# The second pair's v loaded later, behind W1's second piece, and its cast shared by GpSimd and VectorE

## The chip, the cores and the metric

The kernel runs on one core of a Trainium2 chip. The metric is the device time of one execution in microseconds (us); lower is better. TensorE (PE in the profile) multiplies matrices, VectorE (DVE), ScalarE (ACT) and GpSimd (POOL) work on elements, and the core's 16 DMA engines move data between its memories and HBM. Two DMA queues matter here. Loads that SyncE (SP) issues run on the queue that the profile calls q1; loads that GpSimd issues, here those of the weights with a cast from f32 to a 2-byte type on the way, run on q0.

## The reference

A block-wise linear attention with a decay per head, then a normalisation and a two-layer MLP with a residual. B = 4, H = 8 heads, S = 768, D = 64; the MLP goes from 512 to 2048 and back.

```python
for b in range(S // 64):                       # attention, blocks of 64 positions
    intra = (qb @ kb^T) * Dmask                # Dmask[i, j] = lam ** (i - j) where i >= j
    out[:, :, sl] = intra @ vb + (qb * lam_pow) @ kv_state
    kv_state = lam ** 64 * kv_state + (kb * rev_pow)^T @ vb
x = out as (B, S, H * D)
xn = (x - mean) / sqrt(var + 1e-06) * g_ln
result = x + relu(xn @ w_ch1) @ w_ch2
```

## The kernel before

The 4 x 768 positions are cut into 12 windows of 256 positions, `u` = 0 to 11, each one belonging to one batch. The order of all work is written out by hand, and every engine takes its instructions in that order; waits between engines and on DMAs come from what the instructions read and write.

For a window, `load_in` brings q, k and v (512 KB each, as f32 rows of 512 bytes) into buffers, three of each kind. `in_k`, `in_q` and `in_v` turn them into bf16: k is cast, q and v are multiplied by powers of lam and cast. `in_q` with a slice of heads works in two halves, j = 0 and 1, one instruction each (L236). `in_v` is one instruction (L252). `HA` is heads 0 to 3 and `HB` is heads 4 to 7. TensorE then transposes q and k (`transpose_pe`, L260), forms the masked scores (`scores`, L289, masked by VectorE at L299), the products of k with v (`kv`, L333, output `pk`), the outputs of scores and state (`av`, L452, and `inter`, L465, output `po`). `norm` and `to_xT` centre and transpose the result (`xT`).

The first MLP layer takes W1 in four pieces (`load_w1(0)` to `(3)`, L127, issued by GpSimd; 512 KB each as it is stored, in bf16), the second W2 in four pieces (`load_w2`, L130). `m1a.tile(0, i)` uses W1's piece 0 (L689); `m1s(m1a, c, lo, hi)` uses piece c (L571). `m2a(i, part)` uses W2's piece `part` (L715). ScalarE takes the results with a ReLU (`hT`).

The stretch that the change touches runs from about 12 to 24 us. In it, in the order of the program:

- VectorE finishes the masks of window 0, writes one column of window 1's v buffer (the memset of L816), and SyncE then issues window 1's v load (L817): the memset is a gate, since the load writes over the same buffer and so waits for it.
- GpSimd waits on ScalarE's cast of window 1's k (`behind`, L776), issues W1's piece 1 (L894), takes window 1's q for HA (L895), issues pieces 2 and 3 (L897, L898), then casts window 1's v for all heads (L899).
- VectorE takes window 1's q for HB (L896) in two halves, normalises window 0, and masks window 1's scores (L913, L916).
- TensorE runs `m1a.tile(0, 0)`, window 1's scores, `m1a.tile(0, 1)`, the first half of `m1s(m1a, 1)` at L921, which needs W1's piece 1, and then `kv(1)` at L929, which needs window 1's v in bf16.
- ScalarE writes one column of window 2's k buffer (L922), which gates SyncE's loads of window 2's k, q and v; GpSimd's second `behind` (L926) waits for that k to land and then issues W2's pieces.

Of the kernel before, what the change touches and what calls it, by code (L numbers as in the profile page):

```python
# [17 lines left out]
def kernel(  # L18
# [11 lines left out]
    nc = tc.nc  # L30
# [45 lines left out]
    qkv_in = {}  # L76
# [5 lines left out]
    def fill(got, name, u, hs, eng=None):  # L82
        eng = eng or nc.sync
        src = dict(k=k, q=q, v=v)[name]
        if u < LB:
            eng.dma_start(got[:, hs], source(src, u, hs))
            return
        cc, b = divmod(u, B)
        for j in range(2):
            eng.dma_start(got[:, hs, j * D:(j + 1) * D],  # L90
                          src[b, hs, cc * W + j * C:cc * W + (j + 1) * C, :].rearrange("h p d -> p h d"))
# [6 lines left out]
    def open_in(u, gate):  # L98
        qkv_in[u] = {name: inp.tile([128, H, 2 * D], F32, tag=name + "in", name=name + "in") for name in "kqv"}
        if gate:  # L100
            nc.gpsimd.memset(qkv_in[u]["k"][:, 0, 0:1], 0.0)

    def load_in(u, name, eng):
        got = qkv_in[u][name]
        fill(got, name, u, slice(0, H), eng)
        qkv_in[u][name] = got.rearrange("p h (j d) -> p h j d", j=2)
# [19 lines left out]
    def load_w1(c):  # L126
        nc.gpsimd.dma_start(w1[c], moe_w_ch1[:, c * W1C:(c + 1) * W1C].rearrange("(k p) f -> p k f", p=128))  # L127
# [80 lines left out]
    def open_window(u):  # L208
        kq = wk.tile([128, 2, NP, 2, 2, D], BF16, tag="kq", bufs=3, name="kq")
        vb = wk.tile([128, H, 2, D], BF16, tag="vb", bufs=4, name="vb")  # L210
        st[u] = dict(kq=kq, vb=vb)
        if u < XB:
            st[u]["kqT"] = wk.tile([128, 2, NP, 2, 128], BF16, tag="kqT", bufs=3, name="kqT")

    def part(a, dst, hs):

        return dst[:, a, hs.start // 2:hs.stop // 2].rearrange("p a j e d -> p a e j d")

    ALL = slice(0, H)

    def in_k(u, eng, hs=ALL):
        src = qkv_in[u]["k"][:, hs].rearrange("p (a e) j d -> p a e j d", e=2)
        dst = part(0, st[u]["kq"], hs)
        for j in range(2):
            (eng.copy if eng is nc.scalar else eng.tensor_copy)(dst[:, :, :, j], src[:, :, :, j])

    def in_q(u, eng, hs=ALL):
        src = qkv_in[u]["q"][:, hs].rearrange("p (a e) j d -> p a e j d", e=2)
        dst = part(1, st[u]["kq"], hs)
        if u < LB:  # L230
            lq = lam_q[:, hs, :].rearrange("p (a e) j -> p a e j", e=2)
        else:
            lq = lam_p[:, 0:1, hs].rearrange("p j (a e) -> p a e j", e=2).to_broadcast([128, (hs.stop - hs.start) // 2, 2, 2])
        n = (hs.stop - hs.start) // 2
        for j in range(2):
            eng.tensor_tensor(dst[:, :, :, j], src[:, :, :, j],  # L236
                              lq[:, :, :, j:j + 1].to_broadcast([128, n, 2, D]), op=ALU.mult)

    def in_k_one(u, eng, j):
        src = qkv_in[u]["k"].rearrange("p (a e) j d -> p a e j d", e=2)  # L240
        (eng.copy if eng is nc.scalar else eng.tensor_copy)(part(0, st[u]["kq"], ALL)[:, :, :, j], src[:, :, :, j])  # L241
# [7 lines left out]
    def in_v(u, eng, hs=ALL):  # L249
        n = hs.stop - hs.start  # L250
        lv = lam_v[:, hs, :, None] if u < LB else lam_p[:, 1, hs, None, None]
        eng.tensor_tensor(st[u]["vb"][:, hs], qkv_in[u]["v"][:, hs], lv.to_broadcast([128, n, 2, D]), op=ALU.mult)  # L252
# [23 lines left out]
    def scores(u, hf, early=False):  # L276

        s = st[u]
        kT, qT = s["kqT"][:, 0], s["kqT"][:, 1]
        if early:  # L280
            sc = [mm_tile([128, 2, 2, 128], F32, f"sce{e}") for e in range(2)]
        else:
            sc = [bank([128, 2, 2, 128], F32, "sc", f"sc{e}") for e in range(2)]
        mA = wk.tile([128, 2, 2, 2, 128], BF16, tag=f"mA{hf}", name=f"mA{hf}")
        for i in range(2):
            for jk in range(2):
                for ab in range(2):
                    for e in range(2):
                        nc.tensor.matmul(sc[e][half[ab], i, jk, :], lhsT=kT[half[e], 2 * hf + i, jk, half[ab]],  # L289
                                         rhs=qT[half[e], 2 * hf + i, :, half[ab]],  # L290
                                         start=(i == 0 and jk == 0), stop=(i == 1 and jk == 1), skip_group_check=True)
        s[f"mA{hf}"] = mA
        s[f"sc{hf}"] = sc

    def mask(u, hf, heads=(0, 1)):
        s = st[u]
        kp = keep.rearrange("p a b t -> p a (b t)")
        for e in heads:
            nc.vector.tensor_tensor(s[f"mA{hf}"][:, e], s[f"sc{hf}"][e],  # L299
                                    kp[:, None, :, :].to_broadcast([128, 2, 2, 128]), op=ALU.mult)  # L300

    def mask_by_act(u, hf):

        s = st[u]
        for e in range(2):
            nc.scalar.copy(s[f"mA{hf}"][:, e], s[f"sc{hf}"][e])
        kp = keep_h.rearrange("p a b t -> p a (b t)")
        for e in range(2):
            m = s[f"mA{hf}"][:, e]
            nc.vector.tensor_tensor(m, m, kp[:, None, :, :].to_broadcast([128, 2, 2, 128]), op=ALU.mult)  # L310

    def fill_pe(n, tag, wide=False):
        t = bank([128, 128], F32, tag, "unread")
        for i in range(n):
            if wide:
                nc.tensor.matmul(t, lhsT=warm, rhs=warm, start=True, stop=True)
            else:
                nc.tensor.matmul(t[half[i % 2], 0:D], lhsT=warm[half[0], half[i % 2]], rhs=warm[half[0], half[0]],
                                 start=True, stop=True, skip_group_check=True)

    def kv(u, tag="mm", between=None):

        s = st[u]
        cc, b = divmod(u, B)
        n_ab = 2 if (cc + 1) * W < S else 1
        pk = [bank([128, 2, NP, D], F32, f"po{ab}" if tag == "po" else tag, f"pk{ab}")[:, 0] for ab in range(n_ab)]
        for p in range(NP):
            if p == NP // 2 and between:
                between()
            for j in range(2):  # L330
                for e in range(2):
                    for ab in range(n_ab):
                        nc.tensor.matmul(pk[ab][half[e], p, :], lhsT=s["kq"][half[ab], 0, p, j, e],  # L333
                                         rhs=s["vb"][half[ab], 2 * p + e, j],
                                         start=(p == 0 and j == 0), stop=(p == NP - 1 and j == 1), skip_group_check=True)
        s["pk"] = pk
# [434 lines left out]
    HA, HB = slice(0, 4), slice(4, 8)  # L771
# [24 lines left out]
    nc.vector.tensor_copy(e_p[:, 0:1], io_p)  # L796
    nc.vector.tensor_scalar(e_p[:, 1:2], e_p[:, 0:1], -1.0, None, op0=ALU.mult)
    in_q(0, nc.vector, HA)
    in_k(0, nc.gpsimd, HB)
    load_w1(0)  # L800
    in_q(0, nc.vector, HB)
    transpose_pe(0, 1, (0, 1))
    transpose_pe(0, 0, (2, 3), nc.vector)
# [9 lines left out]
    fill_pe(6, "po0")  # L813
    scores(0, 1, early=True)
    mask_by_act(0, 1)
    nc.vector.memset(qkv_in[1]["v"][:, 0, 0:1], 0.0)  # L816
    load_in(1, "v", nc.sync)  # L817
    kv(0, between=lambda: fill_pe(8, "po0"))
    new_state(0, 0, nc.scalar)
    av(0, (0, 1))  # L820
# [46 lines left out]
    def wind_down(u, abs=(0, 1)):  # L867
# [7 lines left out]
        for ab in abs:  # L875
            x, xh = s["x"][:, ab], s["x"][:, ab].rearrange("p (a e d) -> p a e d", e=2, d=D)
            nc.scalar.copy(x, s["po"][ab].rearrange("p h d -> p (h d)"))
            if has[ab]:
# [7 lines left out]
            nc.vector.scalar_tensor_tensor(s["xc"][:, ab], in0=x, scalar=s["mv"][:, ab, 0:1], in1=g_row,  # L886
                                           op0=ALU.subtract, op1=ALU.mult)

    open_window(1)
    in_k(1, nc.scalar)  # L890
    norm(0, 0, early=True)
    reader(0)
    behind(st[1]["kq"][:, 0, 0, 0, 0, 0:1])
    load_w1(1)  # L894
    in_q(1, nc.gpsimd, HA)  # L895
    in_q(1, nc.vector, HB)  # L896
    load_w1(2)  # L897
    load_w1(3)  # L898
    in_v(1, nc.gpsimd)  # L899
    open_in(2, False)  # L900
    fill_pe(5, "sc", True)
    transpose_pe(1, 0, (0, 1))
# [11 lines left out]
    to_xT(0, 1)  # L914
    scores(1, 1, early=True)
    mask(1, 1)  # L916
    for i in range(2):
        nc.scalar.activation(lam_p[:, i], lnlam, ACT.Exp, scale=e_p[:, i:i + 1])
    keep_x(0, nc.scalar.copy)
# [604 lines left out]
```

## Time and profile before

| | |
|---|---|
| time, median of 3 runs | 205.96 us (205.44 to 205.98) |
| the profiled execution's own time | 205.75 us |
| its span, first to last instruction | 204.0 us |
| TensorE busy | 194.7 us, 95% |
| VectorE, ScalarE, GpSimd busy | 142.7, 121.6 and 89.6 us |
| HBM read and written | 27.27 and 6.29 MB |

The profile is of one execution. All points in time below are microseconds from the first instruction, so 1.75 us of the execution's own time lie outside the span. The granted TensorE clock is 1.000 in the whole span. A row of the timeline gives start, duration, engine, line, operation, output and inputs, sizes, and the count of instructions merged into it; a bracket gives the idle time of the engine before it and what ended it. A row of the waits gives in total how long, how often and at most how long one line waited for another. A row of a DMA queue gives its packets, megabytes and the time of its packets as a share of the 16 engines' time in the stretch asked for; since packets overlap, a busy queue can exceed 100%. An issue row ends with the time from issue to landing.

### The profile page before, as it was taken

The page shows a single profiled execution, that of the slowest core. Times are in us where ns is not written, and L with a number is a line of the kernel's source. Part 1 is how long each engine was busy: PE and PEld are TensorE (multiplying, and loading weights), DVE is VectorE, ACT ScalarE, POOL GpSimd, SP SyncE. Part 2 cuts the span into 40 slices and gives each one's busy share as a digit, 9 for nine tenths or more (in the row PEclk, how much of TensorE's full clock was granted, in tenths as well). Part 3 has the DMA queues.
Part 4 walks back from the last instruction along what each step waited for, and adds up shares of the span by engine and source line. Part 5 has one row for each costly group of instructions (what it writes and reads, how often), then busy time and mean ns, then how long its engine had stood idle before and what let it go on. Part 6 is the DMA issues. An engine that isn't in the chain of part 4 may idle for free.

```text
span 204.0 us, 7526 instructions
## 1 busy us (share of the span) xinstructions
PE 194.7 (95%) x3223; PEld 163.0 (80%) x3223; DVE 142.7 (70%) x298; ACT 121.6 (60%) x285; POOL 89.6 (44%) x125
## 2 busy tenths in 40 slices
PE   1998999999999999999999999999999999999992
PEld 0487798645777889889899888888888888888881
DVE  3588372779799879879686576866856577955372
ACT  3787678555425767656596386584484592852720
POOL 5557049301964790863673962644436303001010
PEclk9999999999999999999999999999999999999999
DMA  4999999999989899799699995999989865110703
GB/s 105 302 255 219 217 301 194 196 248 253 231 179 208 186 268 187 156 201 150 145 200 203 210 209 96 213 234 131 190 158 151 249 192 132 29 26 2 203 11 97
DMA packets 93747, 36.41 MB, mean 178 GB/s; under 512 B 71313, under 2 KB 91281, under 8 KB 93714
## 3 DMA queue, kind: packets, MB, share of 16 engines
q1 hardware_dynamic: 88624, 29.96, 69.6%
q0 software_dynamic: 4704, 5.77, 15.4%
q8 instruction: 25, 0.41, 0.8%
q10 hardware_dynamic: 386, 0.20, 0.4%
q14 instruction: 8, 0.07, 0.1%
HBM read 27.27 MB, written 6.29 MB: 164 GB/s over the span
## 4 chain that ended last, share of the span: by engine, by line
PE 77%; DMA 12%; DVE 5%; ACT 3%; POOL 2%; issue 1%; DVEq 0%
PE pm L571 31%; DMA w<-in_moe_w_ch_dram 10%; PE pwd L606 9%; PE pwc L606 9%; PE pwa L606 8%; PE pm1t L689 4%; PE pwb L606 4%; PE pm L715 3%; DMA lam_b<-in_lam_dram 2%; PE po L465 1%; PE po L439 1%; DVE mA L299 1%; PE sc L379 1%; DVE hs L591 1%; PE po L452 1%; PE pk L398 1%
## 5 line engine op out<-in xcount | busy, mean ns | idle before, releaser
L571 PE MATMUL pm<-xT,w 128*128 128x256 bf16 x656 | 76.2, 273 | 0.3 <-DMA w<-in_moe_w_ch_dram 0.3
L571 PEld LDWEIGHTS <-w 128*128 128x128 bf16 x656 | 62.8, 98 | 8.6 <-DMA w<-in_moe_w_ch_dram 0.5
L574 ACT ACTIVATE hT<-pm 128x512 f16<-128x512 f32 x82 | 47.8, 596 | 30.0 <-PE pm L571 28.5
L606 PEld LDWEIGHTS <-hs 128*128 128x128 f16 x320 | 31.1, 98 | 3.6
L631 POOL TENSOR_TENSOR x<-ev_u,x 128x256 f32<-128x256 f32 x10 | 7.4, 742 | 60.4 <-ACT ev_u L630 60.4
L606 PEld LDWEIGHTS <-hT 128*128 128x128 f16 x240 | 23.2, 98 | 2.7
L589 DVE TENSOR_TENSOR hs<-hT 128x1024 f16<-128x1024 f16 x20 | 14.3, 717 | 14.7 <-ACT hT L574 13.5
L508 DVE SCALAR_TENSOR_TENSOR xc<-po,nmean,g_row 128x512 bf16<-128x512 f32 x18 | 13.2, 742 | 5.5 <-ACT nmean L492 5.5
L339 POOL TENSOR_TENSOR Sn<-Stmp,lam_s 128x256 bf16<-128x256 f32 x16 | 10.0, 627 | 13.4 <-DVE Stmp L419 5.6
L715 PE MATMUL pm<-w,hT 128*128 128x512 f16 x64 | 15.1, 379 | 0.1
L491 ACT ACTIVATE x<-po 128x512 f32<-128x512 f32 x18 | 10.7, 594 | 6.6 <-PE po L465 3.7
L689 PE MATMUL pm1t<-xT,w 128*128 128x128 bf16 x224 | 13.7, 219 | 0.6 <-ACT xT L532 0.3
L619 DVE SCALAR_TENSOR_TENSOR x<-pwd,rstd,x 128x256 f32<-128x256 f32 x20 | 9.7, 483 | 6.4 <-POOL x L642 3.4
L689 PEld LDWEIGHTS <-w 128*128 128x128 bf16 x224 | 12.9, 98 | 1.1 <-DMA w<-in_moe_w_ch_dram 0.5
L252 POOL TENSOR_TENSOR vb<-vin,lam_p 128x1024 bf16<-128x1024 f32 x7 | 13.3, 1897 | 0.0
L246 POOL TENSOR_TENSOR kq<-qin,lam_p 128x512 bf16<-128x512 f32 x11 | 11.4, 1043 | 3.8 <-PE pm L571 2.6
L539 ACT ACTIVATE sq<-x,nmean 128x512 bf16<-128x512 f32 x18 | 12.9, 718 | 0.1
L606 PE MATMUL pwa<-w,hT 128*128 128x256 f16 x80 | 12.0, 273 | 0.0
L619 DVE SCALAR_TENSOR_TENSOR x<-pwa,rstd,x 128x512 f32<-128x512 f32 (+1 forms) x20 | 11.5, 611 | 0.7
L606 PE MATMUL pwb<-w,hT 128*128 128x256 f16 x80 | 11.5, 273 | 0.0
L606 PE MATMUL pwd<-w,hs 128*128 128x256 f16 x80 | 11.2, 273 | 0.0
L241 POOL CAST kq<-kin 128x512 bf16<-128x512 f32 x9 | 5.8, 655 | 11.8 <-DMA kin<-in_k_dram 10.6
(139 smaller groups left out, 336.4 us busy)
## 6 DMA issues: line engine op xcount, KB each, us to landing
kin<-in_k_dram SPq DMA_DIRECT2D x16, 256.0 KB, 5.0
qin<-in_q_dram SPq DMA_DIRECT2D x16, 256.0 KB, 4.4
vin<-in_v_dram SPq DMA_DIRECT2D x16, 256.0 KB, 5.1
w<-in_moe_w_ch_dram POOLq DMA_DIRECT2D x8, 512.0 KB, 9.2
out_dram<-x SPq DMA_DIRECT2D x16, 256.0 KB, 4.4
kin<-in_k_dram SPq DMA_DIRECT2D x4, 512.0 KB, 9.7
qin<-in_q_dram SPq DMA_DIRECT2D x4, 512.0 KB, 6.7
vin<-in_v_dram SPq DMA_DIRECT2D x4, 512.0 KB, 7.8
```

Of the source, the lines that this page charges most:

```text
L246: eng.tensor_tensor(part(1, st[u]["kq"], ALL)[:, :, :, j], src[:, :, :, j], lq[:, :, :, None].to_broadcast([128, NP, 2, D]), op=ALU.mult)
L252: eng.tensor_tensor(st[u]["vb"][:, hs], qkv_in[u]["v"][:, hs], lv.to_broadcast([128, n, 2, D]), op=ALU.mult)
L491: nc.scalar.activation(x, po, ACT.Copy, accum_out=sm)
L508: nc.vector.scalar_tensor_tensor(s["xc"][:, ab], in0=po, scalar=s["nmean"][:, ab:ab + 1], in1=g_row, op0=ALU.add, op1=ALU.mult)
L539: nc.scalar.activation(sq, s["x"][:, ab], ACT.Square, bias=s["nmean"][:, ab:ab + 1], accum_out=s["ss"][:, ab:ab + 1])
L571: nc.tensor.matmul(pm[:, b, :], lhsT=w1[n // W2K][:, kk, (n % W2K) * 128:(n % W2K + 1) * 128], rhs=xT_of[g][:, kk, 0:N], start=(b == 0 and ...
L574: nc.scalar.activation(hT[:, u * NB:(u + 1) * NB, 0:N], pm, ACT.Relu)
L589: nc.vector.tensor_tensor(s13, b[:, :, 1:2, :].to_broadcast([128, n, 2, 128]), b[:, :, 0:4:3, :], op=ALU.subtract)
L606: nc.tensor.matmul(pr[bank], lhsT=lhs(r), rhs=rhs, start=(first and r == 0), stop=(r == KB // 2 - 1), skip_group_check=True)
L619: nc.vector.scalar_tensor_tensor(out, in0=in0, scalar=r[ab], in1=in1, op0=ALU.mult, op1=ALU.add)
L689: nc.tensor.matmul(pm[:, b, :], lhsT=w1[c][:, kk, b * 128:(b + 1) * 128], rhs=xT_of[g][:, kk, i * 128:(i + 1) * 128], start=(b == 0 and kk ...
L715: nc.tensor.matmul(acc[i], lhsT=hT[:, kk, i * 128:(i + 1) * 128], rhs=w2[kk // W2K][:, kk % W2K, :], start=(kk == 0), stop=(kk == KB - 1))
```

## The change

The v load of window 1 moves from behind VectorE's last mask of window 0 into the middle of VectorE's `in_q(1)` for HB, memset and load together: `in_q` gets a parameter that is called after its first half. `in_v(1)` on GpSimd is cut to HA and stays where it was; HB goes to VectorE, behind the second mask of window 1.

```diff
-    def in_q(u, eng, hs=ALL):
+    def in_q(u, eng, hs=ALL, after_first=None):
...
         for j in range(2):
             eng.tensor_tensor(dst[:, :, :, j], src[:, :, :, j],
                               lq[:, :, :, j:j + 1].to_broadcast([128, n, 2, D]), op=ALU.mult)
+            if j == 0 and after_first:
+                after_first()
...
     mask_by_act(0, 1)
-    nc.vector.memset(qkv_in[1]["v"][:, 0, 0:1], 0.0)
-    load_in(1, "v", nc.sync)
     kv(0, between=lambda: fill_pe(8, "po0"))
...
+    def late_v():
+
+        nc.vector.memset(qkv_in[1]["v"][:, 0, 0:1], 0.0)
+        load_in(1, "v", nc.sync)
+
     open_window(1)
...
     load_w1(1)
     in_q(1, nc.gpsimd, HA)
-    in_q(1, nc.vector, HB)
+    in_q(1, nc.vector, HB, after_first=late_v)
     load_w1(2)
     load_w1(3)
-    in_v(1, nc.gpsimd)
+    in_v(1, nc.gpsimd, HA)
...
     scores(1, 1, early=True)
     mask(1, 1)
+    in_v(1, nc.vector, HB)
     for i in range(2):
```

## The prediction

> **What bounds the kernel now.** The first view is the list of what TensorE waited for in the whole span, since TensorE is busy for 95% of it.
>
> ```profile
> ...
> PE pm L571 <- DMA w<-in_moe_w_ch_dram: 0.3, 1, 0.3
> PE pm1t L689 <- ACT xT L532: 0.3, 1, 0.3
> PE pm1t L689 <- ACT kqT L261: 0.2, 1, 0.2
> ```
>
> After its start TensorE has three waits, 0.8 us together. They all lie in the stretch that the change touches, as TensorE's timeline shows:
>
> ```profile
> 16.95 1.10 PE L689 MATMUL pm1t<-xT,w 128*128 128x128 bf16 x16 [0.24 <-ACT kqT L261]
> ...
> 19.39 1.05 PE L689 MATMUL pm1t<-xT,w 128*128 128x128 bf16 x16 [0.33 <-ACT xT L532]
> 20.78 1.05 PE L571 MATMUL pm<-xT,w 128*128 128x256 bf16 x8 [0.34 <-DMA w<-in_moe_w_ch_dram]
> 21.76 0.45 PE L333 MATMUL pk<-vb,kq 64*64 64x64 bf16 x32
> ```
>
> At 20.78 it waited 0.34 us for W1's piece 1, and kv(1) at 21.76 follows with no wait. That 0.34 us is what an earlier piece 1 can win here. The chain that ended last shows a second place where weights arrive as TensorE wants them:
>
> ```profile
> 13.39 7.35 DMA w<-in_moe_w_ch_dram
> ...
> 31.26 12.88 DMA w<-in_moe_w_ch_dram
> 44.14 0.04 issue
> 44.18 1.02 PE pm L715 x4
> ```
>
> W2's piece 2, issued at 31.26, lands at 44.14, and the product that needs it starts at 44.18. How long TensorE stood there is seen by comparing two equal groups in its timeline:
>
> ```profile
> 41.00 1.90 PE L715 MATMUL pm<-w,hT 128*128 128x512 f16 x8
> ...
> 43.07 2.13 PE L715 MATMUL pm<-w,hT 128*128 128x512 f16 x8
> ```
>
> The second takes 0.23 us more, the pause at 44.18. So a delay of TensorE before 44 us costs its length less 0.23, and a gain before 44 us is lost unless W2's piece 2 comes earlier too. Behind it TensorE has no wait that the list shows, so what is left goes to the end in full.
>
> **Who holds what in the stretch.** The other engines' timelines:
>
> ```profile
> 12.15 0.06 DVE L816 MEMSET vin<- 128x1 f32 x1
> 12.83 0.70 DVE L497 BATCH_NORM_STATS2 stats<-po 128x6 f32<-128x512 f32 x1 [0.62 <-PE po L452]
> ...
> 14.64 0.49 DVE L236 TENSOR_TENSOR kq<-qin,lam_q 128x256 bf16<-128x256 f32 x1
> ...
> 18.43 1.29 DVE L299 TENSOR_TENSOR mA<-sc,keep 128x512 bf16<-128x512 f32 x2 [0.48 <-PE sc L289]
> 19.64 1.28 DVE L299 TENSOR_TENSOR mA<-sce,keep 128x512 bf16<-128x512 f32 x2
> 24.07 0.17 DVE L476 COPY seen<-po 128x8 f32<-128x8 f32 x1 [3.15 <-PE po L465]
> ```
> ```profile
> 8.02 0.94 POOL L127 DMA_DIRECT2D w<-in_moe_w_ch_dram  x1
> ...
> 13.39 0.80 POOL L127 DMA_DIRECT2D w<-in_moe_w_ch_dram  x1
> 14.21 1.39 POOL L236 TENSOR_TENSOR kq<-qin,lam_q 128x256 bf16<-128x256 f32 x2
> 15.55 1.54 POOL L127 DMA_DIRECT2D w<-in_moe_w_ch_dram  x2
> 18.49 1.90 POOL L252 TENSOR_TENSOR vb<-vin,lam_v 128x1024 bf16<-128x1024 f32 x1 [1.40 <-DMA vin<-in_v_dram]
> 28.07 0.35 POOL L776 COPY seen_p<-kin 128x1 f32<-128x1 f32 x1 [7.67 <-ACT hT L574]
> ```
> ```profile
> 12.25 0.37 SPq L86 DMA_DIRECT2D vin<-in_v_dram  x1
> 22.57 0.37 SPq L86 DMA_DIRECT2D kin<-in_k_dram  x1
> ```
>
> v was issued at 12.25, was there at about 18.4, and was cast from 18.49 to 20.39. kv(1) took it at 21.76, so v has 1.37 us of slack now.
>
> **Part 1, the gate.** The memset (0.06 us) leaves 12.15; VectorE idles for TensorE until 12.83 anyway, so nothing is won. It comes back after the half that ends at 14.64 + 0.49 = 15.13. VectorE has no gap from there until it idles 0.48 us before 18.43, which hides 0.06 us; uncovered it would cost 0.06. SyncE issues v at about 15.2 instead of 12.25, 2.95 us later. On SyncE's queue the next load is at 22.57, so none is pushed back.
>
> **Part 2, when v lands.** This is the term that decides. Three loads share the DMA engines. From issue to landing, piece 0 (issued at 8.02), piece 2 (at 15.55):
>
> ```profile
> w<-in_moe_w_ch_dram POOLq DMA_DIRECT2D x1, 512.0 KB, 8.9
> ...
> w<-in_moe_w_ch_dram POOLq DMA_DIRECT2D x1, 512.0 KB, 7.7
> ```
>
> Piece 0 landed at 16.9, v at 18.4, piece 1 at 13.39 + 7.35 = 20.74, piece 2 at 23.25. On the DMA engine that ends last, the loads follow one another: v costs 18.4 - 16.9 = 1.5 us and piece 1 costs 20.74 - 18.4 = 2.3 us. That they are served in the order of issue, not shared, is seen in the two queues from 17 to 18 us, when piece 1 was long issued:
>
> ```profile
> q0 software_dynamic: 182, 0.19, 112.8%
> q1 hardware_dynamic: 38, 0.02, 6.3%
> ```
>
> 6.3% is one engine of 16, given wholly to v: 0.063 x 16 us / 38 = 27 ns a packet. Now the later stretch from 39 to 43 us, where both queues had much waiting:
>
> ```profile
> q0 software_dynamic: 559, 0.56, 82.7%
> q1 hardware_dynamic: 547, 0.28, 34.6%
> ```
>
> There the queues move packet for packet, and a packet of q1 takes 0.346 x 64 us / 547 = 40 ns. So both ways exist in this trace. I take the order of issue, since the situation is the nearest: the same v, the same pieces of W1, one behind the other. Then piece 1, issued before v, goes first: it lands at 16.9 + 2.3 = 19.2 and v at 19.2 + 1.5 = 20.7. Piece 0's landing, and with it the start at 16.95, stays. The bounds, from the times to landing of all loads of v up to 60 us:
>
> ```profile
> DMA to landing us min/median/max: 5.1/6.2/14.2
> ```
>
> That is 20.3 at the earliest and 29.4 at the latest (the 14.2 us load ran into W2's four pieces). From 15 to 15.75 us q0 did almost nothing:
>
> ```profile
> q0 software_dynamic: 9, 0.01, 5.4%
> ```
>
> Unless piece 1 was only kept out by v, engines that have finished piece 0 now stand still there for up to 0.75 us. Piece 2 lands with 0.7 us in hand before TensorE's next piece of work at about 24, and the engine that ends last has no hole, so I cost this at nothing.
>
> **Part 3, the cast.** The nearest rows are GpSimd's two halves of window 0's v, and VectorE's multiply of the same size:
>
> ```profile
> 8.98 2.06 POOL L252 TENSOR_TENSOR vb<-vin,lam_v 128x512 bf16<-128x512 f32 x2
> ```
> ```profile
> 8.00 0.76 DVE L236 TENSOR_TENSOR kq<-qin,lam_q 128x256 bf16<-128x256 f32 x2 [0.53 <-DMA qin<-in_q_dram]
> 14.64 1.24 DVE L236 TENSOR_TENSOR kq<-qin,lam_q 128x256 bf16<-128x256 f32 x2
> 29.71 0.69 DVE L246 TENSOR_TENSOR kq<-qin,lam_q 128x512 bf16<-128x512 f32 x1 [1.00 <-DMA qin<-in_q_dram]
> ```
>
> HA on GpSimd costs 1.03 us alone. HB on VectorE costs 0.69 alone. Both now run at the same time, and the pair of L236 took 1.24 us beside GpSimd's L236 against 0.76 without it. So HB lies between 0.69 and 0.69 x 1.24 / 0.76 = 1.13, and HA between 1.03 and, with the same 0.48 us, 1.51. I take 1.15 for HA, near the lower end, because the overlap is shorter than HA. VectorE is free at 20.92, so HB ends between 21.6 and 22.1. HA starts 0.1 after the landing: 20.8 + 1.15 = 21.95, and kv(1) can start at about 22.05.
>
> The waits that are added hold up little. Behind HA on GpSimd stands L776, which waits for a load until 28.07. Behind HB on VectorE stands L476 at 24.07, which waits for TensorE's po. ScalarE's gate for window 2's k stands behind the ReLU of L921, not behind kv(1), so W2's loads keep their time.
>
> **The sum.** TensorE could reach kv(1) at 21.76 - 0.34 = 21.42, and the bf16 v lets it start at 22.05: 0.29 us later than before. The pause of 0.23 at 44.18 takes most of it: +0.06. From the profiled execution's 205.75 this gives 205.8; the median of the runs stands 0.21 above that execution, so I forecast 206.0. With HA at its ends and the landing 0.4 us either way, kv(1) starts between 21.5 and 22.8, and the change lies between -0.25 and +0.8: this case's own range is 205.6 to 206.8.
>
> **The rivals.**
>
> *The queues share packet for packet* (slower). Pieces 2 and 3, issued at 15.55 to 17.1, keep q0 full while v runs. By the rows of 39 to 43 us q1 moves 547 packets in 4 us, 137 a us; v has 1024 (512 KB in rows of 512 bytes), 7.5 us. The load issued at 22.57 had its first packets between 23.5 and 23.75:
>
> ```profile
> q1 hardware_dynamic: 20, 0.01, 13.2%
> ```
>
> So from 1.0 us behind its issue, at 16.2, v can run; it ends at 23.7, lands at about 24.2, and kv(1) starts at 25.4: +3.6, less 0.23, gives 209.3 against the median. It decides as soon as W1's piece 2 is taken up before v's packets are. For it: the 39 to 43 rows. Against it: the one engine at 17 to 18 us. The Trainium skill, page "DMA: Bandwidth & Descriptors", section "Queues, rings and completion order", says that each DMA engine goes round between the queues that have work, a packet at a time. By that rule the time would be this rival's; the trace agrees from 39 to 43 us and not at 17 to 18 us.
>
> *Part of v is caught.* If a quarter to a half of v's 64 packets on an engine are paired with piece 2, each costs 4 us x 16 / 547 = 117 ns instead of 27, so 1.4 to 2.9 us more: 207.4 to 208.9, in the middle 208.
>
> *The gain is real.* v lands at 20.3 or sooner, kv(1) starts at 21.42, and W2's piece 2 also comes 0.2 us or more earlier: -0.34 to -0.57, 205.4 to 205.6; if the waits at 16.95 and 19.39 (0.57 together) shrink too, down to 205.0. For it: one DMA engine sets each landing, and the others end sooner. Against it: W2's pieces do not hang on this stretch.
>
> **How the numbers follow.** Forecast 0.50, full sharing 0.16, partial 0.16, gain 0.18. About 0.3%, 0.6 us, is what a measurement can tell from no change. Of the forecast 0.04 lies above that bound, of the gain 0.12 below it. So faster 0.12, within 0.3% 0.46 + 0.06 = 0.52, slower 0.32 + 0.04 = 0.36. The range goes from 205.2 to 208.7, which leaves out most of full sharing and the far end of the gain.
>
> **What would show it.** L571's wait for w at 20.78 gone, its start at about 20.4; GpSimd's half of L252 starting at 20.8; kv(1) at 22.05 with a wait for vb; the pause at 44.18 gone. Wrong if q0 and q1 move equal counts of packets from 18 to 23 us, or if v lands before 20.3.

## The result, and the profile after

| | before | after |
|---|---|---|
| median of 6 runs each | 205.70 us (205.38 to 208.14) | 215.82 us (214.05 to 216.69) |
| profiled execution, its own time | 205.75 | 214.35 |
| its span | 204.0 | 212.6 |
| TensorE's mean granted clock | 1.000 | 0.983 |

The change makes the kernel 4.6% slower: the ratio is 1.0459, with a 95% interval of 1.039 to 1.0527. The forecast was 206.0 us, with 208.7 as the upper end of its range. Ratios here and below leave disturbed runs out; that matters for one experiment, e7, where it drops the four slowest of nine runs although their lower clock may be the edit's own effect.

The two profiled spans differ by 8.6 us. The page of after starts with the span, each engine's busy time, and the granted clock in 40 slices:

```profile
span 212.6 us, 7527 instructions
...
PE 197.0 (93%) x3223; PEld 164.5 (77%) x3223; DVE 146.1 (69%) x299; ACT 121.8 (57%) x285; POOL 88.6 (42%) x125
...
PEclk9999859999999999999999999999999999999999
```

TensorE does the same 3223 instructions but is busy 2.3 us longer (194.7 before), and two slices, from 21 to 32 us, show a lower clock. VectorE is busy 3.4 us longer (142.7 before) with one instruction more. Both are signs that something other than a wait was added. The waits come next, TensorE's list after its start (total, times, longest):

```profile
PE pk L335 <- POOL vb L254: 4.1, 1, 4.1
PE pm L573 <- DVE x L741: 2.8, 1, 2.8
```

Neither wait is in the list of before. The wait for W1's piece 1, which the change was to shorten, is gone. TensorE's timeline of after shows the first one (start, length, engine, line, operation, and in brackets the wait ahead of it):

```profile
20.58 1.04 PE L573 MATMUL pm<-xT,w 128*128 128x256 bf16 x8
25.74 0.64 PE L335 MATMUL pk<-vb,kq 64*64 64x64 bf16 x32 [4.12 <-POOL vb L254]
26.32 1.89 PE L573 MATMUL pm<-xT,w 128*128 128x256 bf16 x8
...
31.51 1.05 PE L573 MATMUL pm<-xT,w 128*128 128x256 bf16 x8
```

The group that was L571 now starts at 20.58 with no wait, 0.20 earlier. kv(1) starts at 25.74 instead of 21.76: **3.98 us of the loss**. Then eight products of L573 take 1.89 us, where eight of the same size take 1.04 at 20.58 and 1.05 at 31.51. The granted clock says why, in two stretches of after (stretch, its length, TensorE's busy time and instructions, granted clock, DMA share, GB/s):

```profile
21.50:24.60 3.10, 0.12 (x2) 1.00 1.24 208
24.60:31.40 6.80, 5.66 (x128) 0.50 1.16 295
```

From 24.6 us, 1.1 us ahead of the end of the pause, the granted clock is half for 6.8 us. What that costs is read where it ends. The L573 group at 31.51 stood at 25.18 before, as the first of these rows of before's timeline shows:

```profile
25.18 1.05 PE L571 MATMUL pm<-xT,w 128*128 128x256 bf16 x8
...
45.04 0.39 PE L531 MATMUL xt<-ident,xc 128*128 128x128 bf16 x4
...
54.17 3.62 PE L715 MATMUL pm<-w,hT 128*128 128x512 f16 x16
```

31.51 - 25.18 = 6.33, so the clock adds 6.33 - 3.98 = **2.35 us**. The Trainium skill, page "TensorE: Matmul & The Clock Gate", section "Why this matters for your kernels", warns of idle gaps of over about 3 us between matmul bursts, after which TensorE falls back to half clock; this trace agrees, with 4.12 us of idling and a clock of 0.50.

The same groups further on, in after:

```profile
49.40 1.90 PE L717 MATMUL pm<-w,hT 128*128 128x512 f16 x8
51.14 0.39 PE L533 MATMUL xt<-ident,xc 128*128 128x128 bf16 x4
...
60.58 2.78 PE L573 MATMUL pm<-xT,w 128*128 128x256 bf16 x24 [2.77 <-DVE x L741]
63.19 3.62 PE L717 MATMUL pm<-w,hT 128*128 128x512 f16 x16
```

The group of L717 at 49.40 stood at 43.07 and took 2.13; now it takes 1.90. The pause of **0.23** for W2's piece 2 is gone, and the transposes behind it are 51.14 - 45.04 = 6.10 late. But the group at 63.19 is 63.19 - 54.17 = 9.02 late, so another 9.02 - 6.10 = **2.92 us** is lost in between, nearly all of it in the 2.77 us wait for VectorE's x. VectorE's timeline of after, ahead of that x:

```profile
51.50 0.83 DVE L840 TENSOR_TENSOR wt<-w 128x512 f16<-128x512 f16 x1
52.36 1.15 DVE L842 TENSOR_TENSOR wt<-w,wt 128x512 f16<-128x512 f16 x1
...
55.82 2.12 DVE L840 TENSOR_TENSOR wt<-w 128x512 f16<-128x512 f16 x1
57.97 0.42 DVE L842 TENSOR_TENSOR wt<-w,wt 128x512 f16<-128x512 f16 x1
...
59.78 0.75 DVE L741 SCALAR_TENSOR_TENSOR x<-pm,rstd,x 128x512 f32<-128x512 f32 x1
```

These are additions of W2's rows, in two groups, and before the same two groups took 0.41 to 0.43 us an addition. The rows that answer to the first two, in VectorE's timeline of before:

```profile
45.14 0.42 DVE L840 TENSOR_TENSOR wt<-w 128x512 f16<-128x512 f16 x1
45.59 0.42 DVE L842 TENSOR_TENSOR wt<-w,wt 128x512 f16<-128x512 f16 x1
```

What lies beside them is GpSimd's work, in its timeline of after and then of before:

```profile
50.69 1.36 POOL L243 CAST kq<-kin 128x512 bf16<-128x512 f32 x2 [2.59 <-DMA kin<-in_k_dram]
52.01 3.60 POOL L248 TENSOR_TENSOR kq<-qin,lam_q 128x512 bf16<-128x512 f32 x3
55.58 2.08 POOL L254 TENSOR_TENSOR vb<-vin,lam_v 128x1024 bf16<-128x1024 f32 x1
```
```profile
51.19 1.36 POOL L241 CAST kq<-kin 128x512 bf16<-128x512 f32 x2 [2.27 <-DMA kin<-in_k_dram]
52.51 3.68 POOL L246 TENSOR_TENSOR kq<-qin,lam_q 128x512 bf16<-128x512 f32 x3
```

GpSimd's multiplies start at about 52 us in both kernels, right behind casts of k that wait for a load of k. VectorE's additions moved from 45 to 51.5 us and now run into these casts and multiplies, and slow down from 0.42 to as much as 2.12 us; the first one after GpSimd's cast of v ends, at 57.66, takes 0.42 again. The Trainium skill, page "SBUF — State Buffer", section "SBUF: two separate sides", says that VectorE and GpSimd share a pair of ports, held by one instruction at a time, when VectorE has two inputs in SBUF; these rows agree, and say how much it is here.

The four terms, 3.98 + 2.35 - 0.23 + 2.92, give 9.02 up to that group by construction, and the span grew by 8.6. Most of the other 0.4 comes back soon behind it: the 64 small products of L452 take 1.00 us at 62.15 in before, and the same ones (L454) take 0.71 at 71.06 in after.

**Why v came late.** The issues of v and of W1, and the first reader of v, are in the timelines of SyncE and of GpSimd, both of after:

```profile
15.12 0.37 SPq L86 DMA_DIRECT2D vin<-in_v_dram  x1
```
```profile
13.32 0.80 POOL L127 DMA_DIRECT2D w<-in_moe_w_ch_dram  x1
...
15.49 1.54 POOL L127 DMA_DIRECT2D w<-in_moe_w_ch_dram  x2
24.21 1.48 POOL L254 TENSOR_TENSOR vb<-vin,lam_v 128x512 bf16<-128x512 f32 x1 [7.18 <-DMA vin<-in_v_dram]
```

v is issued at 15.12, as forecast. It has landed by 24.1, not 20.7. Piece 1, issued 1.8 us ahead of v, did go first, as forecast: from 15 to 18 us q0 moves 411 packets and q1 none, and piece 1 lands 6.5 us behind its issue, at 19.8. The DMA queues of after, packets, MB and share of the engines' time, first from 19 to 20 us and then from 20.75 to 21.5 us:

```profile
q1 hardware_dynamic: 529, 0.27, 90.0%
q0 software_dynamic: 37, 0.03, 20.7%
```
```profile
q0 software_dynamic: 129, 0.13, 104.6%
q1 hardware_dynamic: 45, 0.02, 15.0%
```

In the first stretch v (q1) has nearly all engines to itself, and a packet takes 0.90 x 16 us / 529 = 27 ns. That is half of v's 1024 packets within one microsecond. In the second, W1's pieces 2 and 3 (q0) move and some of v's last packets go in between at 0.15 x 16 x 0.75 us / 45 = 40 ns each. These are the two rates that before showed: 27 ns for a load that an engine serves alone, 40 ns for one that is served in turn with q0. So v isn't shared as a whole, nor served wholly in order: most of it goes at once, and a remainder is paired with piece 2, which was issued 0.37 us behind it. On this reading, which no view shows directly, an engine that has taken v up before piece 2 arrives moves it whole, and the others go in turn. The experiments shift that distance.

### The profile page after: what moved, and what is told of

It is laid out like the page before. It is cut to its first block, busy times and chain, and to the rows that moved or that the text cites. A ratio compares the mean times of both kernels' runs of the same rounds, so it can differ in the third digit from the quotient of the medians.

```text
span 212.6 us, 7527 instructions
## 1 busy us (share of the span) xinstructions
PE 197.0 (93%) x3223; PEld 164.5 (77%) x3223; DVE 146.1 (69%) x299; ACT 121.8 (57%) x285; POOL 88.6 (42%) x125
## 4 chain that ended last, share of the span: by engine, by line
PE 84%; DVE 6%; DMA 5%; ACT 1%; POOL 1%; issue 0%; ACTq 0%; POOLq 0%
PE pm L573 34%; PE pwd L608 8%; PE pwa L608 8%; PE pwc L608 8%; PE pm1t L691 5%; DMA vin<-in_v_dram 4%; PE pwb L608 4%; PE pm L717 4%; PE po L454 2%; PE po L467 2%; PE tp L262 2%; DVE wt L840 1%; DMA g_one<-in_moe_g_ln_dram 1%; PE po L441 1%; PE sc L381 1%; PE pk L335 1%
## 5 line engine op out<-in xcount | busy, mean ns | idle before, releaser
L573 PE MATMUL pm<-xT,w 128*128 128x256 bf16 x656 | 78.0, 276 | 2.8 <-DVE x L741 2.8
L573 PEld LDWEIGHTS <-w 128*128 128x128 bf16 x656 | 63.5, 99 | 11.7 <-issue 2.9
L717 PE MATMUL pm<-w,hT 128*128 128x512 f16 x64 | 15.0, 380 | 0.0
L691 PEld LDWEIGHTS <-w 128*128 128x128 bf16 x224 | 13.3, 100 | 1.2 <-DMA w<-in_moe_w_ch_dram 0.5
L254 POOL TENSOR_TENSOR vb<-vin,lam_v 128x512 bf16<-128x512 f32 (+1 forms) x6 | 9.4, 1575 | 7.2 <-DMA vin<-in_v_dram 7.2
```

Of the source, the lines that this page charges most:

```text
L573: nc.tensor.matmul(pm[:, b, :], lhsT=w1[n // W2K][:, kk, (n % W2K) * 128:(n % W2K + 1) * 128], rhs=xT_of[g][:, kk, 0:N], start=(b == 0 and ...
L691: nc.tensor.matmul(pm[:, b, :], lhsT=w1[c][:, kk, b * 128:(b + 1) * 128], rhs=xT_of[g][:, kk, i * 128:(i + 1) * 128], start=(b == 0 and kk ...
L717: nc.tensor.matmul(acc[i], lhsT=hT[:, kk, i * 128:(i + 1) * 128], rhs=w2[kk // W2K][:, kk % W2K, :], start=(kk == 0), stop=(kk == KB - 1))
```

## The experiments

Theory: three losses hang in a chain. (1) A part of v is paired with W1's piece 2, so kv(1) is late; how much depends on how far ahead of piece 2 v is issued. (2) The pause costs TensorE its clock. (3) The delay pushes VectorE's additions beside GpSimd's multiplies. Rivals: the shared cast is the cost; the pause alone would cost its length in full, without the clock; the moved gate holds something up that the forecast counted as free. Each edit is shown against after unless it says otherwise. The ratios are against the runs of before on the same chip; all numbers of a wait, a clock or a start are of one profiled execution.

**e1: the late load alone**, the cast of v whole on GpSimd as before.

```diff
-    in_v(1, nc.gpsimd, HA)
+    in_v(1, nc.gpsimd)
...
-    in_v(1, nc.vector, HB)
```

> The changed kernel with the cast of window 1's v whole on GpSimd again; only the load is late. Theory (the late landing of v starts everything: v lands at about 24.1, TensorE idles, its granted clock halves, and the shift brings a later wait): v still lands at about 24, GpSimd's whole cast takes 1.9 us instead of 1.48, kv(1) starts near 26.1, the clock drops as in the changed kernel, time 214 to 218 us. Rival (the shared cast, VectorE and GpSimd slowing each other and waiting for v, is a large part of the cost): time falls to 206 to 210 us.

Measured: 215.74 us, ratio 1.049 (1.0423 to 1.0556). kv(1) starts at 26.77 behind a whole cast of 1.90 us, and the clock is 0.983 again. The loss is in the late load, and sharing the cast saves none of it that these runs can tell.

**e2: the shared cast alone**, v loaded as early as before.

```diff
+    nc.vector.memset(qkv_in[1]["v"][:, 0, 0:1], 0.0)
+    load_in(1, "v", nc.sync)
     kv(0, between=lambda: fill_pe(8, "po0"))
...
-    in_q(1, nc.vector, HB, after_first=late_v)
+    in_q(1, nc.vector, HB)
```

> The kernel before with only the cast of window 1's v shared: HA on GpSimd, HB on VectorE behind the second mask; the load where it was. Theory (late landing is all): v lands at about 18.4, HA ends by 20.0, HB by 21.7, kv(1) starts within 0.2 us of 21.76, time within 0.3% of the kernel before (205.2 to 206.4 us). Rival (the shared cast costs): 208 us or more.

Measured: 205.64 us, ratio 0.9983 (0.9948 to 1.0018). The cast costs nothing that can be measured. kv(1) missed what was expected: it starts at 22.59, because W1's piece 1 came late in this execution (a wait of 1.30 us ahead of L573), although neither load was moved against before; the runs don't show why. GpSimd's timeline of e2 also shows what its half costs when VectorE's half isn't beside it:

```profile
18.16 1.04 POOL L254 TENSOR_TENSOR vb<-vin,lam_v 128x512 bf16<-128x512 f32 x1 [1.13 <-DMA vin<-in_v_dram]
```

In after, with VectorE's half at the same time, it took 1.48.

**e3: TensorE kept busy.** Eighteen products whose result nobody reads stand ahead of kv(1). v still comes late, but TensorE doesn't idle.

```diff
+    keep_busy(18, "po0")
     kv(1, "sc")
```

> The changed kernel with 18 products of 128x512 that nobody reads in front of kv(1), about 3.9 us of TensorE work in the place where it idled. Theory (the idle of 4.1 us halves the granted clock for 6.8 us, which costs 2.8 us): v and kv(1) as in the changed kernel (about 24.1 and 25.8), the clock stays 1.0 and the products behind kv(1) run in 1.05 us for 8, not 1.9; time 2.8 us less, about 212 to 213; if the later wait of 2.8 us for VectorE needed the whole shift of 6 us, it shrinks too: down to 209. Rival (the clock drop has another cause than the idle time, or the slow products another cause than the clock): unchanged, 214 to 217 us.

Measured: 211.46 us, ratio 1.0268 (1.0215 to 1.0322), 4.4 us less than after. TensorE's timeline of e3:

```profile
21.17 4.05 PE L785 MATMUL idle<-keep_h,ident 128*128 128x512 bf16 x18
25.15 0.45 PE L335 MATMUL pk<-vb,kq 64*64 64x64 bf16 x32
25.53 1.05 PE L573 MATMUL pm<-xT,w 128*128 128x256 bf16 x8
```

kv(1) is still 3.39 late, and eight products take 1.05 again. The clock was a loss of its own. The wait for VectorE's x is down to 1.4 us. Here the eighteen products, not v, set kv(1): v had landed when GpSimd began its half at 22.48. That is earlier than in after, with the same order of issues, 0.37 us apart as well.

**e4: W1's pieces 2 and 3 held back.** GpSimd issues them behind the first LayerNorm's statistics, so v has a longer lead.

```diff
     in_q(1, nc.vector, HB, after_first=late_v)
-    load_w1(2)
-    load_w1(3)
-    in_v(1, nc.gpsimd, HA)
...
     st[0]["tmp"] = state_sum(0, 1)
+    behind(st[0]["mv"][:, 1, 0:1])
+    load_w1(2)
+    load_w1(3)
+    in_v(1, nc.gpsimd, HA)
```

> The changed kernel with GpSimd issuing W1's pieces 2 and 3 some 1.4 us later, behind VectorE's bn_aggr of window 0's second half (near 16.9 instead of 15.5). Theory (on the DMA engines where piece 2's packets arrive before all of v's have been taken up, the rest of v is paired packet for packet with piece 2): v is taken up whole before piece 2 arrives, lands between 20.2 and 21.5, kv(1) starts at 21.5 to 22.6, the clock stays 1.0, time 205 to 207 us. Rival (v lands late because it is issued 2.9 us later and its own queue is slow, whatever stands in q0): v lands at 23 or later, time 212 us or more.

Measured: 206.51 us, ratio 1.005 (1.0025 to 1.0074). GpSimd's timeline of e4:

```profile
17.16 1.54 POOL L127 DMA_DIRECT2D w<-in_moe_w_ch_dram  x2
21.74 1.54 POOL L254 TENSOR_TENSOR vb<-vin,lam_v 128x512 bf16<-128x512 f32 x1 [3.04 <-DMA vin<-in_v_dram]
```

v, issued at 15.44, has 1.72 us of lead and is there by 21.7. kv(1) starts at 23.33, behind a pause of 1.70 us that leaves the clock at 1.0, and VectorE is in time. v and kv(1) are later than expected, but nearly the whole loss goes with the position of pieces 2 and 3 alone. What is left, 0.9 us in the span, is less than kv(1)'s delay of 1.57.

**e5: GpSimd held behind VectorE's additions.** Its multiply of window 3's q waits until the additions of W2's pieces 1, 2 and 0 are done.

```diff
-    in_q_one(3, nc.gpsimd, 0)
...
     w_sums(0, 1)
+    behind(wt[0][:, 0, 3, 0:1])
+    in_q_one(3, nc.gpsimd, 0)
```

> The changed kernel with GpSimd's multiplies of windows 3's and 4's q (and the v cast behind them) held back until VectorE's weight sums of W2's pieces 1, 2 and 0 are done. Theory (TensorE's wait of 2.8 us for VectorE near 60 us comes from those sums running beside GpSimd's multiplies, 0.8 to 2.1 us each instead of 0.42): the sums take 0.42 us each, the wait is under 0.5 us, time 212 to 213.5 us. Rival (VectorE is late because TensorE's results come late, whatever GpSimd does): the wait stays at 2 us or more, 215 to 217 us. A new wait for window 3's q could eat part of the gain; it would show as TensorE waiting for the scores of window 3.

Measured: 210.99 us, ratio 1.0274 (1.022 to 1.0328). VectorE's timeline of e5, then GpSimd's:

```profile
52.79 0.41 DVE L840 TENSOR_TENSOR wt<-w 128x512 f16<-128x512 f16 x1
53.24 0.43 DVE L842 TENSOR_TENSOR wt<-w,wt 128x512 f16<-128x512 f16 x1
...
54.71 1.27 DVE L840 TENSOR_TENSOR wt<-w 128x512 f16<-128x512 f16 x1
```
```profile
54.46 3.44 POOL L248 TENSOR_TENSOR kq<-qin,lam_q 128x512 bf16<-128x512 f32 x3
```

While GpSimd stands still the additions take 0.42 us; as it starts at 54.46, the one at 54.71 takes 1.27. TensorE's wait for x is gone. The median, 4.8 us below after's, lies below the expected range, and the gain is larger than the 2.9 that this term has in the profile of after. Between the two profiled spans it is 3.8 us, close to 2.92 for the wait and 1.16 for the clock, whose half spell lasted 3.4 us here, by chance and not by the edit, less 0.19 for a later kv(1). The rest lies in the scatter of the runs: after's profiled execution is 1.5 us below its median.

**e6: both cures together**, fourteen products ahead of kv(1) and the hold of e5.

```diff
+    keep_busy(14, "po0")
     kv(1, "sc")
...
-    in_q_one(3, nc.gpsimd, 0)
...
     w_sums(0, 1)
+    behind(wt[0][:, 0, 3, 0:1])
+    in_q_one(3, nc.gpsimd, 0)
```

> The changed kernel with 14 unread products (3.0 us of TensorE work) in front of kv(1), and GpSimd's multiplies held back as in the run before. Theory (three terms that add up: late v, halved clock, VectorE's sums beside GpSimd): only the late v is left. kv(1) starts at 24.3 to 25.8, the clock stays 1.0, the wait for VectorE is under 0.5 us, time 207.5 to 209.5 us. Rival (a further term is hidden behind these): 211 us or more.

Measured: 209.17 us, ratio 1.0165 (1.012 to 1.021). TensorE's timeline of e6:

```profile
26.61 0.44 PE L335 MATMUL pk<-vb,kq 64*64 64x64 bf16 x32 [2.12 <-POOL vb L254]
```

In this execution v came later still than expected, and kv(1) is 26.61 - 21.76 = 4.85 late; the eight products behind it take 1.05. With the clock and VectorE's wait out of the way that is all that is left: 4.85 - 0.23 = 4.62, less the 0.29 that L454 gives back here too, against 4.2 in the span. So a late kv(1) costs about its length, and the other two losses come on top.

**e7: the gate ahead of VectorE's cast of q** instead of in its middle.

```diff
-    in_q(1, nc.vector, HB, after_first=late_v)
+    late_v()
+    in_q(1, nc.vector, HB)
```

> The changed kernel with the gate in front of VectorE's first half of q instead of between the halves: v is issued 0.45 us earlier, still behind W1's piece 1. Theory (v's packets that are not yet taken up when piece 2's arrive are paired with them): more of v gets in ahead; fewer paired packets than 135, v lands between 21 and 23, kv(1) 22.3 to 24.5, the clock stays 1.0, time 206.5 to 210 us. Rival (v just follows its issue): v lands 0.45 us earlier, 23.6, and the clock still drops: 213 us or more.

Measured: all nine runs have a median of 209.05 us, 1.5% above before's 205.91, and lie between 206.52 and 216.62; the ratio is 1.0102 (1.0052 to 1.0152). v is issued at 14.94, piece 2 at 15.71, a lead of 0.77. TensorE's timeline, and the clock in two stretches, both of e7:

```profile
23.35 0.62 PE L335 MATMUL pk<-vb,kq 64*64 64x64 bf16 x32 [2.38 <-POOL vb L254]
23.90 1.89 PE L573 MATMUL pm<-xT,w 128*128 128x256 bf16 x8
```
```profile
20.97:23.35 2.38, 0.00 (x0) 1.00 1.24 207
23.35:26.80 3.45, 3.45 (x112) 0.51 1.19 265
```

The landing came as expected, kv(1) at 23.35. That the clock would hold was wrong: 2.38 us of idling cost it here, for 3.45 us, though 2.12 in e6 and 1.70 in e4 didn't. The Trainium skill, page "TensorE: Matmul & The Clock Gate", section "Why this matters for your kernels", names gaps of over about 3 us; this run lost the clock after less, and that decides.

**e8: W1 without its gate.** GpSimd's first wait, ahead of piece 1, is left out, so that piece 1 is issued earlier.

```diff
     reader(0)
-    behind(st[1]["kq"][:, 0, 0, 0, 0, 0:1])
     load_w1(1)
```

> The changed kernel without GpSimd's wait for ScalarE's cast of window 1's k in front of W1's piece 1, so that pieces 1 is issued near 11 us instead of 13.3 (pieces 2 and 3 stay behind window 1's q). Theory: piece 1 follows piece 0 with no hole, v follows it and is taken up before piece 2 arrives; v lands between 19.5 and 21.5, kv(1) 21.5 to 23, time 205 to 207 us. Rival (the pairing does not depend on when q0 has work ahead of v): v lands at 23 or later, 212 us or more.

Measured: 215.21 us, ratio 1.0475 (1.0407 to 1.0543), a clear miss. GpSimd's timeline of e8, then its queues from 20.75 to 21.5 us:

```profile
14.45 1.54 POOL L127 DMA_DIRECT2D w<-in_moe_w_ch_dram  x2
26.78 1.48 POOL L254 TENSOR_TENSOR vb<-vin,lam_v 128x512 bf16<-128x512 f32 x1 [10.79 <-DMA vin<-in_v_dram]
```
```profile
q0 software_dynamic: 104, 0.10, 81.0%
q1 hardware_dynamic: 109, 0.06, 35.7%
```

The edit moved pieces 2 and 3 up as well, to 14.45, so piece 2 is now 0.69 us ahead of v (issued at 15.14). q0 and q1 move packet for packet, and a packet of v takes 0.357 x 16 x 0.75 us / 109 = 39 ns. v lands 2.6 us later than in after. Of all runs this one comes nearest to a full pairing.

**e9: e8 with pieces 2 and 3 held back as in e4.** Piece 1 is issued at 11.01, v at 15.11, piece 2 at 16.67.

```diff
     reader(0)
-    behind(st[1]["kq"][:, 0, 0, 0, 0, 0:1])
     load_w1(1)
...
-    load_w1(2)
-    load_w1(3)
-    in_v(1, nc.gpsimd, HA)
...
     st[0]["tmp"] = state_sum(0, 1)
+    behind(st[0]["mv"][:, 1, 0:1])
+    load_w1(2)
+    load_w1(3)
+    in_v(1, nc.gpsimd, HA)
```

> The run with W1's piece 1 issued near 11 us once more, but with pieces 2 and 3 held to 16.9 us by VectorE's bn_aggr. In that run pieces 2 and 3 had come 1.0 us earlier too, at 14.45 and 15.24, in front of v at 15.14, and nearly all of v was paired. Theory (only pieces 2 and 3, and when they are issued against v, decide): v is issued 1.8 us ahead of piece 2, few packets are paired, v lands between 19.8 and 21.5, kv(1) starts 21.4 to 23, the clock stays 1.0, time 205 to 206.8 us. Rival (an early piece 1 by itself makes v late): v lands at 23 or later, 212 us or more.

Measured: 206.55 us, ratio 1.0039 (1.0014 to 1.0065), with kv(1) at 21.80. GpSimd's timeline of e9:

```profile
20.71 1.04 POOL L254 TENSOR_TENSOR vb<-vin,lam_v 128x512 bf16<-128x512 f32 x1 [2.49 <-DMA vin<-in_v_dram]
```

The same early piece 1 as in e8, and v lands 6 us sooner. It is the place of pieces 2 and 3 that decides. The cast shows one thing more: here GpSimd's half starts 0.08 us ahead of VectorE's and takes 1.04, as in e2, while VectorE's takes 1.50; in after VectorE's half starts first, at 24.10, and keeps its 0.69, while GpSimd's takes 1.48.

**e10: e9 with v loaded early again**, at 12.43, and the cast shared; an attempt to be faster than both kernels. Against e9:

```diff
+    nc.vector.memset(qkv_in[1]["v"][:, 0, 0:1], 0.0)
+    load_in(1, "v", nc.sync)
     kv(0, between=lambda: fill_pe(8, "po0"))
...
-    in_q(1, nc.vector, HB, after_first=late_v)
+    in_q(1, nc.vector, HB)
```

> The run e9 with v's load back at 12.2 us where it was before the change; the cast stays shared. A try at a kernel that beats both: piece 1 at 11.0 and v at 12.2 follow piece 0 with no hole. Theory (kv(1) needs both piece 1 and a v that is cast, and the pause for W2's piece 2 near 44 us takes back what comes before): v lands between 18 and 20.9, piece 1 between 18.5 and 20.8, kv(1) starts 21.2 to 22.2; time within 0.3% of the kernel before, 205.2 to 206.4 us. Rival (what is won in front of kv(1) reaches the end): 205.0 us or less.

Measured: 205.47 us, ratio 1.0001 (0.9984 to 1.0018). kv(1) starts at 21.96. No version here beats the kernel before by more than the runs scatter.

Put side by side, v's lead over piece 2 and the time from v's issue to GpSimd's first read of it:

| | e8 | after | e7 | e9 | e4 |
|---|---|---|---|---|---|
| lead, us | -0.69 | 0.37 | 0.77 | 1.56 | 1.72 |
| issue to first read, us | 11.64 | 9.09 | 6.88 | 5.60 | 6.30 |

At 0.37 us the executions scatter: 9.57 in e1, 7.23 in e3, 9.12 in e5, 9.69 in e6. The other columns are one execution each.

## Why the prediction was wrong

- **Where v is issued** (15.2, measured 15.12), that the gate on VectorE costs nothing, and that no load behind it on SyncE's queue is pushed back: right.
- **W1's piece 1 comes sooner, its wait goes** (L571 at 20.4): right, 20.58 without a wait. It was of no use, because kv(1) waits behind it.
- **When v lands**: this step failed. It took the order of issue and got 20.7; it is 24.1. Of these 3.4 us, 0.6 are piece 1, which went first but landed at 19.8, not 19.2. The prediction took up the one engine that served v alone and concluded that a load waits only for what was issued ahead of it. It left out that piece 2, issued 0.37 us behind v, has a claim as well. In before v led piece 2 by 15.55 - 12.25 = 3.30 us, so that row couldn't show it. With pieces 2 and 3 issued later the landing was 20.7 (e9) and 21.7 (e4). The sentence on piece 2 asked whether *it* had time in hand, not what it does to v.
- **The cast** (HA at 1.15): 1.48, close to the upper bound of 1.51. The reason given for the lower value, an overlap shorter than HA, was wrong; the cast took 0.44 us more than alone in e2, beside a VectorE half that started first. It is 0.33 of the error.
- **The pause at 44.18**: right, it went, 0.23.
- **"A delay of TensorE before 44 us costs its length less 0.23"**: this step failed too. It holds where TensorE keeps its clock and VectorE isn't pushed beside GpSimd: in e6 4.85 cost 4.2, in e4 1.57 cost 0.9, each also less the 0.3 at L452 that the list of waits doesn't show. In after the same sentence misses 2.35 us of clock and 2.92 us of VectorE. Neither stood in the sum or in any rival, and they are more than half of the 8.6.
- **The rivals.** *Part of v is caught* had the mechanism: most of v alone, a remainder in turn with piece 2. It gave 207.4 to 208.9, because its delay of 1.4 to 2.9 us is short of the 3.4 measured and, above all, because it priced the delay only by its length. *Packet for packet* was what e8 showed, not after; its kv(1) at 25.4 comes near by another way. *The gain is real* is ruled out by the landing at 24.1, and e10, with v and piece 1 both early, gained nothing either.
- **What would show it**: neither of the two signs of being wrong came, though it was wrong. From 18 to 23 us q1 moved 1029 packets and q0 650, and v didn't land before 20.3. A v that goes mostly alone and whose last packets go in turn fits neither.
- **The range** ended at 208.7 because all of the cases used the same price for a delay. With the clock and VectorE in the sum, a kv(1) at 25.74 gives 205.75 + 9.02 = 214.8, where 214.35 was measured. The lower end of the forecast's own range holds a slip, since 0.25 below 205.96 is 205.7 and not 205.6; nothing hangs on it.

Two things stay open: why v's landing scatters between 22.4 and 25.0 us with the same 0.37 us of lead, and whether an engine really takes a load up whole. The second is argued from the packet times and from the five leads, not seen. Nor do the runs separate piece 2 from piece 3, which is issued right behind it and moved with it.

## What to carry to other kernels

When a load is moved, ask which transfer will be issued right *behind* it, not only which is ahead: here 0.77 us of lead over another queue's transfer instead of 0.37 came with 0.4 to 2.8 us less from issue to first read, and 0.77 ahead instead of 0.69 behind with 4.8 less. And don't price a stall of the busiest engine by its length alone: look up how long it will stand idle, for its clock, and which engines' work moves with it while other work, timed by loads, stays in place, since the two may come to lie side by side.

## What the runs showed of the hardware that wasn't expected

- The half clock came in spells of 3.4 us (e5), 3.45 (e7), 6.8 (after) and 10.2 (e8, where TensorE idles through the first part of it). It came after a pause of 2.38 us in e7, and not after 2.12 in e6 or 1.70 in e4.
- Additions of two 2-byte tiles on VectorE take 0.42 us alone and 0.83 to 2.12 us beside GpSimd's casts and multiplies (e5 shows 0.42 and 1.27 within 2 us of one trace). Where the two engines' halves of v's cast overlap, the one that starts first keeps its time: 0.69 on VectorE against 1.48 on GpSimd in after, 1.04 on GpSimd against 1.50 on VectorE in e9.
- A packet of v takes 27 ns where an engine serves it alone and 39 to 40 ns in turn with q0. Since each such packet then waits for one of W1's, the remainder of v costs far more than these 13 ns suggest.
